# Fewer transfers for the remaining rows of a batch: six in place of ten

## The chip, the cores and the metric

One NeuronCore of a Trainium2 chip. The metric is device time in microseconds (us) of one execution of the whole program on that core. In the profile the engines are PE (TensorE, matmuls), PEld (its weight loads), DVE (VectorE), ACT (ScalarE), POOL (GpSimd) and SP (SyncE, which here only issues transfers). Each engine works through its own instruction list in order; SPq and ACTq are rows in which SP or ACT issues a transfer.

## The reference, cut to what matters

Three stages in a row, all in float32: sparse attention per head, a gated feed-forward layer, and a Fourier mixing with a channel network. B = 4 batches, S = 576 positions, D = 512 features.

```python
# attention: scores under (row maximum - tau) are dropped, softmax, times v
x = attn_out.transpose(0, 2, 1, 3).reshape(B, S, D)
# feed-forward ("FFN")
xk = mu_k * x + (1 - mu_k) * x_prev ; xr likewise with mu_r
k  = maximum(xk @ w_k, 0)
x  = sigmoid(xr @ w_r) * ((k * k) @ w_v)
# Fourier mixing and channel network
mixed = real(fft(fft(x, axis=1), axis=2))
u  = x + mixed
un = (u - mean(u)) / sqrt(var(u) + 1e-6)
out = u + maximum(un @ w_ch1, 0) @ w_ch2
```

## The kernel before

**Stages.** Attention runs to about 510 us of the profile. The FFN goes on behind it for the batches 2 and 3 until about 617 us (matmuls into `kps` with w_k, `rps` with w_r, `vps` with w_v), and beside it run the Fourier stages of batches 0 and 1. From about 617 us on the channel network (`mixer`, matmuls into `c1ps` and `c2ps`) fills PE, and beside it run the Fourier stages of batches 2 and 3.

**The Fourier stage of one batch.** The FFN's output lies in DRAM as `xd[b]`, 577 rows of 512 floats: row s holds position s up to 287, row 288 + s holds the mirror position 576 - s, and row 576 (again in row 288) the middle position 288. `fft_fold(b)` loads a row and its mirror row to the same partition of two tiles. Two pairs of 128 rows come by `load_pairs` (tiles `xa`, `xb`). What is left, 32 rows and the middle row, comes by `load_rem` into two tiles `ra` and `rb` of 98 partitions each: the 32 rows stand there three times (partitions 0 to 31, 33 to 64 and 65 to 96) and the middle row twice (32 and 97), since one matmul of 98 rows then takes the high and low parts of data and table at once. `folded` makes sums and differences of them: ACT copies `fp<-ra` (L776) and `fq<-rb` (L777), and adds on DVE (L778 to L781). `stack_tile` rounds them into `ske` and `sko`: ACT L793, DVE L794. In `stage_1` (`fft_one`), the matmuls with the cosine table `tc1` and the sine table `ts1` (L802 to L804) collect into `f`, and the matmul L805 with `ske` or `sko` closes each sum. The tables are loaded by POOL (L746) at the start of batch 0.

**What sets the order.** The program is written as generators that are interleaved (`side` next to the FFN, `behind` next to the mixer). The order on each engine is then set by a scheduler that goes by priorities and its own estimate of when operands are there. So a change of a few transfers also moves rows on PE, DVE, ACT and SP that have nothing to do with them. All engines are in order: an ACT row that waits for a transfer holds up all ACT rows behind it. The c1ps, kps, rps and vps sums share two PSUM buffers (`psm`); each is emptied by an ACT row: `relu` (L473) for kps, `hh` (L1100) for c1ps.

**Queues and lanes.** `xa`, `xb`, `ra`, `rb` and the reloads of the mixer are issued by SP; the channel weights `wraw` (L56) and the FFN's stores `xd<-xnat` (L558) by ACT. Transfers of SP and ACT share eight completion counters, called lanes here (DMAHW0 to DMAHW7 in the order listings). Before a transfer is issued, the issuing engine waits for the transfer that used the same lane before.

**Buffers.** `ra` and `rb` take two of the four buffers with tag "o"; the normed inputs `un` and the FFN's `xnat` are in the same four. In batch 2, the tiles must wait until the transposes of `un` on PE (L1005) have read theirs.

Of the kernel before, what the change touches and what calls it, by code (L numbers as in the profile page):

```python
# [20 lines left out]
D, FF, FC = 512, 1024, 2048  # L21
# [8 lines left out]
def tile_kernel(ctx: ExitStack, tc: tile.TileContext, a):  # L30
    nc = tc.nc
    pe, dve, act, pool, sp = nc.tensor, nc.vector, nc.scalar, nc.gpsimd, nc.sync
# [5 lines left out]
    xd = [dram.tile([S + 1, D], F32, name=f"xd{b}") for b in range(B)]  # L38
# [722 lines left out]
    def load_rem(b):  # L761

        xa = chp.tile([128, D], F32, tag="o", bufs=4, name="ra")[:98]
        xb = chp.tile([128, D], F32, tag="o", bufs=4, name="rb")[:98]
        for r in (0, 33, 65):
            sp.dma_start(xa[r:r + 32], xd[b][256:288, :])
            sp.dma_start(xb[r:r + 32], xd[b][544:576, :])
        for r in (32, 97):
            sp.dma_start(xa[r:r + 1], xd[b][576:577, :])
            sp.dma_start(xb[r:r + 1], xd[b][576:577, :])  # L770
        return xa, xb

    def folded(xa, xb, n):
# [76 lines left out]
    def fft_fold(b):  # L850
        while written[b] < 2:
            yield
        settle()
        prs = prs_of[b] = load_pairs(b)
        ra, rb = load_rem(b)
        parts_e, parts_o = [], []
        for xa, xb in prs:
            e, o = folded(xa, xb, 128)
            yield
            parts_e.append(split_tile(e, 257, "fse"))  # L860
            parts_o.append(split_tile(o, 256, "fso"))
            yield
        e, o = folded(ra, rb, 98)
        yield
        ske = stack_tile(e, 257, "ske")
        sko = stack_tile(o, 256, "sko")
        fold_of[b] = (parts_e, parts_o, ske, sko)
        yield
# [495 lines left out]
```

## Time and profile before

| | us |
|---|---|
| median of 3 runs | 1053.23 |
| the three runs | 1051.57 to 1055.49 |
| profiled execution, time | 1055.04 |
| profiled execution, span | 1053.0 |
| granted TensorE clock, mean | 0.989 |
| PE busy in the span | 1003.0 (95%) |
| DVE, ACT, POOL busy | 717.3, 536.3, 395.4 |

The span is what the trace covers; 2.04 us lie around it. Times within the trace count from the span's start. "Granted clock" is 1.00 where TensorE runs at the upper of its two levels (2.4 GHz) and 0.50 at the lower (1.2 GHz). Rows of SPq and ACTq are issues of transfers, not the transfers; where a transfer ends is read from who waited for it.

### The profile page before, as it was taken

The numbers are of one execution on the slowest core, as the hardware profiler recorded it, in microseconds if no ns is written. First come the engines' busy times: TensorE is split into PE (matmuls) and PEld (weight loads), VectorE is DVE, ScalarE is ACT, GpSimd is POOL, SyncE is SP. The second block draws the span as 40 slices with busy tenths as digits, with TensorE's granted clock in tenths as the row PEclk, the third lists the DMA queues.
The fourth block names the chain that finished last, engine by engine and source line by source line (L and its number), as shares of the span: only waits on it lengthen the run. The fifth ranks groups of instructions, "written<-read, shape, count | busy, mean of one in ns | idle before, by whom it ended". The sixth has DMA issues, their size and how long they took to land.

```text
span 1053.0 us, 18827 instructions
## 1 busy us (share of the span) xinstructions
PE 1003.0 (95%) x6807; PEld 884.1 (84%) x6807; DVE 717.3 (68%) x1880; ACT 536.3 (51%) x1211; POOL 395.4 (38%) x495
## 2 busy tenths in 40 slices
PE   6887779999999999999999989999999999999998
PEld 4565659988889888999889879898998888889997
DVE  6799988667776685865356889457537449236776
ACT  4688777675866766857265745243313113113332
POOL 1445868465584564844233100000014125112231
PEclk9899989999999999999999989999999999999999
DMA  6442332121211212100613666536325335223221
GB/s 228 146 133 80 118 108 60 48 67 43 72 60 48 73 31 88 51 24 14 198 55 110 202 204 200 159 127 207 119 92 180 130 119 175 96 101 120 101 100 61
DMA packets 45636, 114.52 MB, mean 109 GB/s; under 512 B 6319, under 2 KB 6740, under 8 KB 45544
## 3 DMA queue, kind: packets, MB, share of 16 engines
q1 hardware_dynamic: 27920, 74.47, 22.2%
q10 hardware_dynamic: 12344, 22.13, 6.8%
q0 software_dynamic: 5280, 16.72, 4.4%
q8 instruction: 54, 0.88, 0.4%
q14 instruction: 38, 0.31, 0.1%
HBM read 84.98 MB, written 28.32 MB: 108 GB/s over the span
## 4 chain that ended last, share of the span: by engine, by line
PE 74%; DVE 10%; DMA 6%; ACT 3%; issue 3%; POOL 2%; SPq 0%; ACTq 0%; DVEq 0%; POOLq 0%
PE c1ps L1090 7%; PE c1ps L1089 6%; PE c1ps L1088 6%; PE s L227 5%; PE av L388 5%; PE c2ps L1112 5%; PE c2ps L1110 5%; PE c2ps L1111 5%; PE p L1045 4%; PE t L329 4%; PE kps L408 2%; PE kps L409 2%; PE kps L410 2%; DMA rawqk<-in_qk 2%; PE vps L530 2%
## 5 line engine op out<-in xcount | busy, mean ns | idle before, releaser
L267 DVE TENSOR_REDUCE small<-s 128x1 f32<-128x576 f32 x144 | 106.9, 752 | 48.1 <-PE s L227 37.3
L1159 POOL DMA_DIRECT2D ud<-u x54 | 29.5, 546 | 264.2 <-DVE u L1158 206.3
L290 POOL TENSOR_SCALAR e<-e,small 128x576 f32<-128x576 f32 x112 | 90.1, 811 | 87.9 <-DVE small L637 73.5
L282 DVE SCALAR_TENSOR_TENSOR e<-s,small,e 128x576 f32<-128x576 f32 x128 | 102.7, 812 | 25.6 <-ACT e L278 22.4
L278 ACT ACTIVATE e<-s,small 128x576 f32<-128x576 f32 x128 | 93.9, 745 | 31.1 <-DVE small L267 27.9
L1100 ACT ACTIVATE hh<-c1ps 128x256 fp32r<-128x256 f32 (+1 forms) x84 | 37.1, 443 | 137.2 <-PE c1ps L1090 111.6
L1101 DVE SCALAR_TENSOR_TENSOR hh<-c1ps,hh 128x256 fp32r<-128x256 f32 (+1 forms) x84 | 41.6, 496 | 89.2 <-ACT hh L1100 89.2
L329 PE MATMUL t<-ident,e 128*128 128x128 f32 x512 | 82.5, 278 | 12.9 <-ACT pt L332 6.5
L332 ACT ACTIVATE pt<-t 128x512 f32<-128x512 f32 x128 | 75.2, 599 | 22.3 <-PE t L329 20.6
L329 PEld LDWEIGHTS t<-ident,e 128*128 128x128 f32 x512 | 61.2, 142 | 24.3 <-issue 6.9
L488 POOL TENSOR_TENSOR k<-relu,k 128x288 fp32r<-128x288 f32 x64 | 54.3, 851 | 68.1 <-ACT k L486 63.9
L408 PE MATMUL kps<-xh,wk 128*128 128x288 f32 x256 | 78.1, 306 | 1.7 <-DVE tg L537 0.9
L530 PE MATMUL vps<-k,wv 128*128 128x288 f32 x256 | 77.5, 304 | 0.4 <-ACT tg L518 0.4
L531 PE MATMUL vps<-k,wv 128*128 128x288 f32 x256 | 77.3, 303 | 0.0
L532 PE MATMUL vps<-k,wv 128*128 128x288 f32 x256 | 76.7, 301 | 0.0
L410 PE MATMUL kps<-xh,wk 128*128 128x288 f32 x256 | 76.2, 298 | 0.0
L409 PE MATMUL kps<-xl,wk 128*128 128x288 f32 x256 | 76.2, 298 | 0.0
L1090 PE MATMUL c1ps<-ut,cB 128*128 128x256 f32 (+1 forms) x256 | 76.0, 297 | 0.0
L1089 PE MATMUL c1ps<-ut,cB 128*128 128x256 f32 (+1 forms) x256 | 75.8, 296 | 0.0
L1088 PE MATMUL c1ps<-ut,cB 128*128 128x256 f32 (+1 forms) x256 | 75.7, 296 | 0.0
L1088 PE MATMUL c1ps<-ut,cA 128*128 128x256 f32 (+1 forms) x224 | 71.0, 317 | 1.4 <-ACT ut L1008 1.4
L1089 PE MATMUL c1ps<-ut,cA 128*128 128x256 f32 (+1 forms) x224 | 70.7, 316 | 0.0
(270 smaller groups left out, 3116.4 us busy)
## 6 DMA issues: line engine op xcount, KB each, us to landing
u<-ud SPq DMA_DIRECT2D x36, 512.0 KB
wraw<-in_w_ch ACTq DMA_DIRECT2D x64, 256.0 KB
rawqk<-in_qk SPq DMA_DIRECT2D x24, 608.0 KB
ud<-u POOLq DMA_DIRECT2D x54, 256.0 KB, 2.5
v<-in_v SPq DMA_DIRECT2D x16, 320.0 KB
un<-ud SPq DMA_DIRECT2D x18, 256.0 KB
out<-u SPq DMA_DIRECT2D x18, 256.0 KB
wraw<-in_w_k SPq DMA_DIRECT2D x8, 512.0 KB
```

The costliest lines, as they stand in the source:

```text
L267: dve.tensor_reduce(st[:, 0:1], sps[n][:, :, 0:HS], axis=AX.XY, op=ALU.max, negate=True)
L278: act.activation(two(eview(n)), sps[n][:, :, 0:HS], AF.Exp, bias=st[:, 0:1])
L282: dve.scalar_tensor_tensor(e, sps[n][:, :, 0:HS], st[:, 1:2], e, op0=ALU.is_ge, op1=ALU.mult, accum_out=st[:, 2:3])
L290: pool.tensor_scalar(e, e, st[:, 2:3], 1.0, op0=ALU.mult, op1=ALU.mult)
L329: pe.transpose(t[:, k, :], e[:, o + 128 * k:o + 128 * (k + 1)], ident)
L408: pe.matmul(ps, wh, x[0][k], start=(k == 0), stop=False)
L409: pe.matmul(ps, wh, x[1][k], start=False, stop=False)
L410: pe.matmul(ps, wl, x[0][k], start=False, stop=(k == nk - 1))
L530: pe.matmul(ps, wv[0][:, c:c + 128], k2[0][:, k, :], start=(k == 0), stop=False)
L1088: pe.matmul(ps, wh, ut[0][:, k, :], start=(k == 0), stop=False)
L1089: pe.matmul(ps, wh, ut[1][:, k, :], start=False, stop=False)
L1090: pe.matmul(ps, wl, ut[0][:, k, :], start=False, stop=(k == 3))
```

## The change

In `load_rem` the ten transfers per batch become six. For each of `ra` and `rb` one transfer fills the partitions 33 to 96: it reads the 32 source rows twice, through an access pattern whose first dimension has two steps of stride zero. One fills the partitions 0 to 31 as before. One fills the partitions 32 and 97 with the middle row, again through a pattern that repeats its source twice. The bytes that arrive are the same: 98 rows of 2 KB in each tile. All three transfers of `ra` are now issued ahead of those of `rb`; before, they alternated.

```diff
         xa = chp.tile([128, D], F32, tag="o", bufs=4, name="ra")[:98]
         xb = chp.tile([128, D], F32, tag="o", bufs=4, name="rb")[:98]
-        for r in (0, 33, 65):
-            sp.dma_start(xa[r:r + 32], xd[b][256:288, :])
-            sp.dma_start(xb[r:r + 32], xd[b][544:576, :])
-        for r in (32, 97):
-            sp.dma_start(xa[r:r + 1], xd[b][576:577, :])
-            sp.dma_start(xb[r:r + 1], xd[b][576:577, :])
+        for x, r in ((xa, 256), (xb, 544)):
+            rows = xd[b][r:r + 32, :]
+            sp.dma_start(x[33:97], rows.rearrange("(a p) d -> a p d", a=1).to_broadcast([2, 32, D]))
+            sp.dma_start(x[0:32], rows)
+            sp.dma_start(x[32:98:65], xd[b][576:577, :].to_broadcast([2, D]))
         return xa, xb
```

The file is one line shorter, and in the listings of the order after the change every line from L768 of before on has a number that is lower by one: L776 is L775, L805 is L804, L1100 is L1099.

On ACT in batch 0, from the issue of a weight load on, with what each row waits for (DMAHW: a lane; PE, DVE, Pool, Activation: a counter of that engine). Before:

```order
L56 DMA wraw<-in_w_ch 128x512 [waits DMAHW4_49,DMAHW2_49,DVE_49]
L777 ACTIVATE fq<-xb 128x2 [waits DMAHW7_49]
...
L473 ACTIVATE relu<-kps 128x288 [waits PE_49]
L556 ACTIVATE xnat<-xn 128x512 [waits PE_49]
L479 ACTIVATE relu<-relu 128x288 [waits Activation_49]
L558 DMA xd_65<-xnat 128x512 [waits DMAHW4_49,Activation_49]
L486 ACTIVATE k_6363<-relu 128x288 [waits Activation_49]
L776 ACTIVATE fp<-ra 98x2 [waits DMAHW5_49,DMAHW7_49,DMAHW1_49,DMAHW0_49]
L473 ACTIVATE relu<-kps 128x288 [waits PE_49,Pool_49]
L479 ACTIVATE relu<-relu 128x288 [waits Activation_49]
L777 ACTIVATE fq<-rb 98x2 [waits DMAHW6_49,DMAHW3_49,DMAHW0_49]
```

With the change:

```order
L56 DMA wraw<-in_w_ch 128x512 [waits DMAHW7_49,DMAHW4_49,DVE_49]
L776 ACTIVATE fq<-xb 128x2
...
L473 ACTIVATE relu<-kps 128x288 [waits PE_49]
L775 ACTIVATE fp<-ra 98x2 [waits DMAHW3_49,DMAHW1_49,DMAHW0_49]
L556 ACTIVATE xnat<-xn 128x512 [waits PE_49]
L479 ACTIVATE relu<-relu 128x288 [waits Activation_49]
L558 DMA xd_65<-xnat 128x512 [waits Activation_49]
L486 ACTIVATE k_6359<-relu 128x288 [waits Activation_49]
L776 ACTIVATE fq<-rb 98x2 [waits DMAHW6_49,DMAHW5_49,DMAHW4_49]
L473 ACTIVATE relu<-kps 128x288 [waits PE_49,Pool_49]
L479 ACTIVATE relu<-relu 128x288 [waits Activation_49]
L792 ACTIVATE ske<-fy 98x257 [waits DVE_49]
```

The weight load no longer waits for lane 2, which in the order before carries the third transfer of `ra` and `rb`, but for lane 7, which carries a transfer of `xb`. `fp<-ra` has moved ahead of an eviction (xnat), and `fq<-rb` ahead of the next relu eviction of kps.

On PE in batch 0, behind the second group of transposes `xn<-ident,tg`. Before (24 kps matmuls stand between, of which the last three are shown):

```order
L408 MATMUL kps<-xh,wk_86 128x288
L409 MATMUL kps<-xl,wk_86 128x288
L410 MATMUL kps<-xh,wk_87 128x288
L805 MATMUL f_6503<-tc1r,ske 128x290
L805 MATMUL f_6513<-ts1r,sko 128x288
```

With the change:

```order
L548 MATMUL xn<-ident,tg 128x128 x4
L804 MATMUL f_6499<-tc1r,ske 128x290
L408 MATMUL kps<-xh,wk_86 128x288
L409 MATMUL kps<-xl,wk_86 128x288
L410 MATMUL kps<-xh,wk_87 128x288
...
L804 MATMUL f_6509<-ts1r,sko 128x288
L408 MATMUL kps<-xh,wk_86 128x288
```

The matmul with `ske` has moved ahead by 24 kps matmuls, to directly behind the transposes; that with `sko` by 12.

On ACT in batch 2, from the copies of the transposed `un` on (`ut`; `cB<-wbits` rounds a weight piece). Before:

```order
L1008 ACTIVATE ut_7808<-ut 128x4x128 [waits PE_49] x2
L75 ACTIVATE cB_7703<-wbits 128x256 [waits DVE_49]
L56 DMA wraw<-in_w_ch 128x512 [waits DMAHW2_49,DMAHW0_49]
L1100 ACTIVATE hh<-c1ps 128x256 [waits PE_49,Activation_49]
L987 ACTIVATE lnst<-lnst 128x2 [waits DVE_49,Activation_49]
L75 ACTIVATE cB_7703<-wbits 128x256 [waits DVE_49]
L56 DMA wraw<-in_w_ch 128x512 [waits DMAHW6_49,DMAHW1_49]
L1100 ACTIVATE hh<-c1ps 128x256 [waits PE_49]
L776 ACTIVATE fp<-ra 98x2 [waits DMAHW4_49,DMAHW5_49,DMAHW3_49,DMAHW1_49]
L75 ACTIVATE cB_7703<-wbits 128x256 [waits DVE_49]
L56 DMA wraw<-in_w_ch 128x512 [waits DMAHW0_49]
L777 ACTIVATE fq<-rb 98x2 [waits DMAHW7_49,DMAHW5_49,DMAHW3_49]
```

With the change:

```order
L1007 ACTIVATE ut_7800<-ut 128x4x128 [waits PE_49] x2
L775 ACTIVATE fp<-ra 98x2 [waits DMAHW5_49,DMAHW4_49,DMAHW3_49]
L1099 ACTIVATE hh<-c1ps 128x256 [waits PE_49,Activation_49]
L986 ACTIVATE lnst<-lnst 128x2 [waits DVE_49,Activation_49]
L776 ACTIVATE fq<-rb 98x2 [waits DMAHW7_49,DMAHW6_49,DMAHW0_49]
L75 ACTIVATE cB_7695<-wbits 128x256 [waits DVE_49]
L56 DMA wraw<-in_w_ch 128x512 [waits DMAHW2_49]
L75 ACTIVATE cB_7695<-wbits 128x256 [waits DVE_49]
L56 DMA wraw<-in_w_ch 128x512 [waits DMAHW1_49]
L1099 ACTIVATE hh<-c1ps 128x256 [waits PE_49]
```

`fp<-ra` now stands directly behind the copies of `ut`; before, two evictions `hh` came first. `fq<-rb` has one `hh` ahead of it in place of two.

## Rows read from the trace of the kernel before

**Rows 1.** The page, part 1: busy us (share) x instructions

```profile
PE 1003.0 (95%) x6807; PEld 884.1 (84%) x6807; DVE 717.3 (68%) x1880; ACT 536.3 (51%) x1211; POOL 395.4 (38%) x495
```

**Rows 2.** PE in time order, batch 0, idle time before in brackets

```profile
523.02 0.37 PE L802 MATMUL f<-ts,fsoh 128*128 128x288 f32 x1 [1.51 <-DMA ts<-in_ts]
...
526.00 0.41 PE L802 MATMUL f<-tc,fseh 128*128 128x290 f32 x1 [0.31 <-ACT fseh L787]
...
527.50 0.40 PE L804 MATMUL f<-ts,fsol 128*128 128x288 f32 x1 [0.34 <-DVE fsol L788]
...
531.66 0.40 PE L408 MATMUL kps<-xh,wk 128*128 128x288 f32 x1
...
534.95 0.29 PE L805 MATMUL f<-tc1r,ske 98*128 98x290 f32 x1
```

**Rows 3.** The chain of work, 505 us on: start us, us, what

```profile
513.74 4.91 DMA ra<-xd
518.65 5.34 issue
```

**Rows 4.** Stretches: us, engines' busy us, PEclk, DMA share, GB/s

```profile
510.00:527.00 17.00, 15.18 (x111) 14.50 (x109) 8.25 (x23) 3.95 (x14) 4.71 (x8) 1.00 1.10 313
...
617.00:624.00 7.00, 5.38 (x24) 5.09 (x25) 5.42 (x13) 4.01 (x9) 0.00 (x0) 0.51 0.98 327
640.00:660.00 20.00, 20.00 (x132) 18.19 (x131) 17.95 (x59) 9.03 (x23) 1.08 (x2) 1.00 0.75 220
...
527.00:528.00 1.00, 0.66 (x5) 0.50 (x4) 0.45 (x1) 0.92 (x3) 0.17 (x1) 1.00 0.11 36
512.00:514.00 2.00, 2.00 (x17) 2.00 (x16) 0.26 (x1) 0.21 (x1) 2.00 (x4) 1.00 1.07 386
```

**Rows 5.** The tile ra: its issues on SP, ns min/median/max

```profile
L766 SPq DMA_DIRECT2D ra<-xd x12: 302/414/487, 511.7 to 650.3; - x12
```

**Rows 6.** ACT in time order, batch 0: start us, us, line, out<-in

```profile
528.13 0.19 ACT L776 ACTIVATE fp<-ra 98x2 f32<-98x2 f32 x1
...
530.39 0.19 ACT L777 ACTIVATE fq<-rb 98x2 f32<-98x2 f32 x1
```

**Rows 7.** DVE in time order, batch 0

```profile
532.84 0.42 DVE L794 TENSOR_TENSOR ske<-fy,ske 33x257 fp32r<-33x257 f32 x1 [0.27 <-ACT ske L793]
```

**Rows 8.** SP's queue in time order, batch 2

```profile
639.07 1.25 SPq L766 DMA_DIRECT2D ra<-xd  x3
```

**Rows 9.** The page, part 6: KB each, us from issue to landing

```profile
ud<-u POOLq DMA_DIRECT2D x54, 256.0 KB, 2.5
```

**Rows 10.** ACT in time order, batch 2

```profile
640.17 0.60 ACT L1008 ACTIVATE ut<-ut 128x512 fp32r<-128x512 f32 x1 [0.53 <-PE ut L1005]
...
646.06 0.20 ACT L776 ACTIVATE fp<-ra 98x2 f32<-98x2 f32 x1
...
646.46 0.20 ACT L777 ACTIVATE fq<-rb 98x2 f32<-98x2 f32 x1
```

**Rows 11.** PE in time order, batch 2

```profile
646.51 0.28 PE L1088 MATMUL c1ps<-ut,cA 128*128 128x256 f32 x1
...
648.86 0.28 PE L1088 MATMUL c1ps<-ut,cA 128*128 128x256 f32 x1
...
657.22 0.30 PE L805 MATMUL f<-tc1r,ske 98*128 98x290 f32 x1
```

**Rows 12.** SP in time order, batch 1

```profile
539.22 0.21 SPq L770 DMA_DIRECT2D rb<-xd  x1
```

**Rows 13.** ACT in time order, batch 1

```profile
564.20 0.21 ACT L776 ACTIVATE fp<-ra 98x2 f32<-98x2 f32 x1 [0.23 <-DVE fsel L788]
```

**Rows 14.** ACT in time order, batch 3

```profile
690.11 0.19 ACT L776 ACTIVATE fp<-ra 98x2 f32<-98x2 f32 x1
```

**Rows 15.** PE in time order, end of the FFN

```profile
615.13 0.76 PE L548 MATMUL xn<-ident,tg 128*128 128x128 f32 x5 [1.43 <-DVE tg L537]
...
618.20 0.58 PE L1088 MATMUL c1ps<-ut,cA 128*128 128x256 f32 x1 [1.45 <-ACT ut L1008]
```

## The prediction

> **What bounds the kernel now.** The first view was the page's first part: PE is busy 95% of the span, the next engine 68% [rows 1]. So a gain has to come from PE's idle time or its clock, and a loss is whatever makes PE wait. The change touches four places, one per batch, and I read PE in time order around each. At batch 0, three waits stand: 1.51 us for the sine table `ts`, 0.31 for `fseh`, 0.34 for `fsol` [rows 2]; the matmuls with `ske` at 534.95 follow their neighbours without a wait. The chain of work shows where the short ones come from: it runs through the third transfer of the remaining rows, from 513.74 for 4.91 us, and then 5.34 us of "issue" on ACT [rows 3]. By the listing of the order, that is the weight load L56 standing on lane 2 until this transfer has landed, at 518.65 + 5.34 = 523.99. All ACT work of the fold queues behind it, `fseh` and `fsoh` too. At batch 2 PE has no wait: all 20 us of 640 to 660 are busy [rows 4].
>
> **What is removed.** On SP an issue of 32 rows takes 0.41 us [rows 5]; four fewer per batch are 1.7 us at most. They lie on SP, which computes nothing, and PE waits for no issue in these stretches; I cost them at nothing. If issues did stand on the path, up to 1.7 us per batch would be the gain. The larger removal is the ACT wait: L56 now stands on a lane that a transfer of `xb` used, issued ahead of all these. That can give back 0.31 + 0.34 = 0.65 us in batch 0; the 1.51 for the table stay, since POOL's loads don't change.
>
> **What the new transfers cost.** No row of before shows a transfer that reads its source twice. The lower bound is that they run as the 32-row ones do, spread over all sixteen DMA engines: then the same bytes take the same time and the cost is nothing. The upper bound is that the dimension of two, which stands outermost in the 64-row and the 2-row patterns, is what is dealt out to the engines, so that only two of sixteen carry them. The weight is then not in the sum of bytes but in two queues: 64 rows x 2048 B = 131 kB per tile, 65.5 kB on each of the two engines, for both tiles 131 kB, plus 4 kB from the 2-row transfers and 8 from the 32-row ones, 143 kB. Before, these engines had a sixteenth of 196 x 2048 B, 25 kB. So 118 kB more on two engines. I take this bound, because the access pattern as written has nothing but the two to deal out in front, and the change put it there in place of a dimension of 32.
>
> The Trainium skill says the same as a rule: in "DMA: Bandwidth & Descriptors", section "Rules for kernel authors", a leading zero-stride broadcast of c copies confines the whole DMA to at most c engines. No row of before shows it, as said. Its row on many small transfers in the same section speaks for the change (below 64 KB mostly overhead); by that one the sum would be a gain of up to 1.7 us per batch if SP's issues were on the path, which no row here bears out.
>
> **Batch 0.** In 510 to 527 the DMA engines are saturated (share 1.10): 313 GB/s x 17 us = 5.32 MB, 333 kB per engine. At 527 they fall to 0.11 [rows 4]. Their rate when full: 386 GB/s / 16 = 24.1 kB per us and engine. The extra 118 kB keep two engines busy 118 / 24.1 = 4.9 us longer, and `rb`, last in SP's queue, lands at about 531.9; before, `fp<-ra` ran at 528.13 and `fq<-rb` at 530.39 [rows 6], when neither was waited for. From `fq<-rb` to the end of the low part of `ske` on DVE are 532.84 + 0.42 - 530.39 = 2.9 us [rows 6, 7]. So `ske` is ready at 534.8. In the new order PE wants it directly behind the transposes, where kps goes on at 531.66 in before [rows 2], and no longer at 534.95: the 24 kps matmuls (3.2 us) that would have covered the delay now stand behind it. PE loses 534.8 - 531.66 = **3.1 us**. The 0.65 us of the ACT wait are no separate gain then: PE would only reach the wait earlier. Behind the late `fp<-ra` stand the eviction `xnat`, and behind `fq<-rb` the next `relu`, so part of the loss will show as PE waiting for ACT. Bounds: -0.65 (sixteen engines) and about +6 (the clock falls as well, below).
>
> **Batch 2.** SP issues from 639.07 [rows 8]. A store of 256 KB over sixteen engines lands in 2.5 us [rows 9]; 16 kB at 24.1 are 0.7, which leaves 1.8 us from issue to landing beside the bytes. The DMA engines are at 0.75 there [rows 4]. If the two engines serve these bytes all of the idle quarter and half of the rest, they get 0.625 x 24.1 = 15 kB/us: 4.4 us for a tile, 8.7 for both. `ra` lands at 639.3 + 4.4 + 1.8 = 645.5, `rb` at 649.8. ACT in the new order reaches `fp<-ra` right behind the copies of `ut`, that is from 640.8 on, where before it came at 646.06 and `fq<-rb` at 646.46 [rows 10]. The first `hh` behind it comes out at about 646.1; PE needs its buffer for the third c1ps group at 646.51 [rows 11], so no loss. The second `hh` stands behind `fq<-rb` and two roundings `cB` of 0.42: 649.8 + 0.2 + 0.84 + 0.38 = 651.2, and the fourth group, which starts at 648.86 in before, must wait for it: **2.4 us**. `ske` itself is wanted at 657.22 [rows 11] and is no issue. Bounds: at the full rate `rb` lands at 646.5 and the loss is nothing; at half rate it is 4.5; if the two engines have only their idle quarter, 6 kB/us, it is about 15. The middle is nearest to the row on the share, so I take it.
>
> **Batches 1 and 3, and the order.** Batch 1's last transfer is issued at 539.22 [rows 12] and `ra` used at 564.20 [rows 13]; batch 3's last 32-row transfer of `ra` is issued at 650.3 [rows 5] and `ra` used at 690.11 [rows 14]. Even 15 us more are covered there; without this cover the price would be that of batch 2 each. The scheduler also reorders DVE and ACT at the end of the FFN. There PE waits 1.43 us for `tg` and 1.45 for `ut` [rows 15], and behind these waits the granted clock is 0.51 for 7 us with 5.38 us of PE work [rows 4]; at full clock the same work takes 5.38 x 0.51 = 2.7, so 2.6 us are lost. DVE's last `tg` has about seven operations fewer ahead of it, but batch 1's `make_u` runs later; I set this at 0, with -5.5 (1.43 + 1.45 + 2.6) and +3 as bounds.
>
> **Sum.** 3.1 + 2.4 + 0 = +5.5 us. Against the profiled execution, whose 1055.04 us are its 1053.0 of span and 2.04 around it, that is 1060.5. The median of the three runs lies 1.81 below the profiled one, so I state the time against it: 1053.23 + 5.5 = **1058.7 us**.
>
> **The rivals.**
> - *No cost, no gain.* The new transfers are spread over all sixteen engines like the old, or the two engines' queue is hidden. For it: no row of before shows the confinement, and batches 1 and 3 have cover. Against: the new order takes the cover away in batches 0 and 2. Gain 0.65: 1052.6.
> - *Faster, through the wait for `tg`.* Transfers cost nothing and the reordering brings `tg` 1.43 us or more earlier at 613. The point that decides is whether the idle time before 617 shrinks enough that the clock stays at 1.00 as it does behind the 1.51 us wait at 523 [rows 2, 4]. Then 0.65 + 1.43 + 1.45 + 2.6 = 6.1 us are gained: 1047.1. Against: later `make_u` rows on the same engine.
> - *Slower by more.* The two engines, and in batch 0 the waits for the table and for `ra` and `rb` add up to where the clock falls as at 617 (+2.6), or batch 2 runs at half rate or less (4.5 and more in place of 2.4). 1058.7 + 2.6 + 2.1 = 1063.4, and up to 1071 at a quarter of the rate.
>
> **Chances.** A difference of 0.5%, 5.3 us, is about what a measurement of this kernel can tell from none: 1047.9 and 1058.5 are the limits. The forecast's case (two engines, 1054 to 1062) has 0.50, of which 0.21 lie under the limit; no cost 0.19; the gain at `tg` 0.12, of which 0.10 under 1047.9; slower by more 0.19. Faster 0.10, same 0.21 + 0.19 + 0.02 = 0.42, slower 0.29 + 0.19 = 0.48. The range that leaves out most of the `tg` case and the end of the last case is 1050 to 1066.
>
> **What would show it.** Right: in batch 0 PE waits 2 to 4 us in the stretch 527 to 535 for `ske`, `xn` or kps, released by ACT or by `ra`/`rb`; ACT shows idle time before `fp<-ra` or `fq<-rb`, released by their transfers, in batch 0 and in batch 2; DMA share behind 527 stays small but above zero (two of sixteen is 0.12) until about 532; the 5.34 us of "issue" are gone. Wrong: if ACT runs `fp<-ra` of batch 2 right behind `ut` without a wait, the transfers aren't confined and the first rival holds. If the transfers are late and PE still doesn't wait, the cover is larger than I read it. If the stretch 612 to 624 differs by more than 3 us, the order decides and not the transfers.

## The result and the profile after

| | before | after |
|---|---|---|
| median of six runs each, us | 1053.82 | 1065.40 |
| lowest to highest, us | 1051.57 to 1055.49 | 1062.53 to 1067.73 |
| ratio, 95% interval | | 1.0109 [1.0089, 1.013] |
| profiled execution: time, span, us | 1055.04, 1053.0 | 1067.73, 1065.8 |
| granted clock, mean | 0.989 | 0.985 |

The change costs 11.5 us (0.0109 x 1053.8), more than twice the 5.5 that were forecast. In the runs below, one execution of e7 (3436.52 us) and one of e8 (2503.97 us) are slow ones and are left out of medians and ratios. The profiled execution is the slowest of the six, and 12.8 us longer in its span than that of before, of which 6.5 are more busy time of PE [rows 1]; the number of matmuls is the same.

```profile
PE 1009.5 (95%) x6807; PEld 887.1 (83%) x6807; DVE 715.4 (67%) x1880; ACT 535.9 (50%) x1211; POOL 395.7 (37%) x495
```

The chain of work from 505 us on shows the new wait. Where [rows 3] had 4.91 us of a transfer and 5.34 of "issue", `rb` now holds the chain for 13.43 us, down to the fold:

```profile
510.99 7.75 DMA wraw<-in_w_ch
518.75 13.43 DMA rb<-xd
...
532.31 0.42 DVE fp L777
```

The stretches after, and then those of before (us, busy us of PE, PEld, DVE, ACT, POOL, PEclk, DMA share, GB/s):

```profile
520.00:525.00 5.00, 4.09 (x32) 3.88 (x31) 3.20 (x7) 2.07 (x7) 0.81 (x1) 1.00 1.24 316
525.00:530.00 5.00, 2.73 (x23) 2.50 (x20) 0.00 (x0) 1.10 (x4) 0.00 (x0) 1.00 0.37 108
530.00:535.00 5.00, 2.95 (x18) 2.26 (x18) 2.38 (x7) 3.09 (x10) 1.41 (x2) 1.00 0.23 76
535.00:540.00 5.00, 5.00 (x26) 5.00 (x27) 1.38 (x3) 2.97 (x8) 1.40 (x3) 0.66 0.31 104
527.00:528.00 1.00, 0.72 (x6) 0.49 (x4) 0.00 (x0) 0.00 (x0) 0.00 (x0) 1.00 0.14 49
...
536.00:538.00 2.00, 2.00 (x10) 2.00 (x10) 0.20 (x1) 0.49 (x3) 0.80 (x1) 0.50 0.56 179
...
650.00:651.00 1.00, 0.04 (x1) 0.04 (x1) 0.06 (x1) 0.57 (x3) 0.00 (x0) 1.00 0.13 49
664.00:666.00 2.00, 2.00 (x14) 1.53 (x12) 1.71 (x6) 0.47 (x2) 0.00 (x0) 1.00 0.11 38
668.00:672.00 4.00, 3.05 (x14) 3.01 (x14) 3.85 (x9) 0.41 (x1) 1.08 (x2) 0.57 1.00 282
```

```profile
520.00:525.00 5.00, 3.49 (x27) 3.29 (x26) 0.72 (x2) 0.60 (x3) 0.00 (x0) 1.00 1.34 291
525.00:530.00 5.00, 4.35 (x29) 3.72 (x29) 3.18 (x6) 3.48 (x10) 1.61 (x2) 1.00 0.60 179
530.00:535.00 5.00, 4.88 (x38) 4.64 (x37) 2.66 (x6) 4.48 (x13) 1.60 (x2) 1.00 0.39 118
535.00:540.00 5.00, 5.00 (x40) 4.80 (x40) 1.28 (x3) 3.77 (x12) 1.61 (x2) 1.00 0.15 33
```

Three things are to be seen. From 527 to 528, and from 650 to 651 in batch 2, the transfer engines are 0.14 and 0.13 busy and move 49 GB/s: two of sixteen (0.125), at some 24 GB/s each. PE is busy 14.77 us of 520 to 540, where it was 17.72: 2.95 less. And from 535 to 540 it is busy throughout, but at 0.66 of its clock; the stretch 536 to 538 lies at 0.50, the lower level. That gives away 5 x 0.34 = 1.7 us more. The sum, 4.6, is what a fixed point behind it shows: the first matmul into `rps` starts at 547.79 and not at 543.16 (0.26 of it was there before batch 0: a `vps` row at 516.93 stood at 516.67).

PE in time order, with the idle time before a row and its releaser:

```profile
529.99 0.41 PE L408 MATMUL kps<-xh,wk 128*128 128x288 f32 x1 [2.27 <-ACT xnat L556]
...
532.85 0.66 PE L548 MATMUL xn<-ident,tg 128*128 128x128 f32 x4 [0.99 <-ACT relu L473]
534.49 0.40 PE L804 MATMUL f<-tc1r,ske 98*128 98x290 f32 x1 [0.99 <-DVE ske L793]
...
620.29 0.77 PE L548 MATMUL xn<-ident,tg 128*128 128x128 f32 x5 [0.65 <-DVE tg L537]
...
623.36 0.38 PE L1087 MATMUL c1ps<-ut,cA 128*128 128x256 f32 x1 [1.45 <-ACT ut L1007]
...
650.96 0.50 PE L1109 MATMUL c2ps<-cA,hh 128*128 128x512 f32 x1 [1.29 <-ACT hh L1099]
...
654.50 0.50 PE L1109 MATMUL c2ps<-cA,hh 128*128 128x512 f32 x1 [0.45 <-ACT hh L1099]
...
655.70 0.39 PE L1087 MATMUL c1ps<-ut,cA 128*128 128x256 f32 x1 [0.46 <-DVE hh L1100]
...
659.25 0.50 PE L1109 MATMUL c2ps<-cA,hh 128*128 128x512 f32 x1 [0.89 <-DVE u L1157]
...
667.54 0.50 PE L1087 MATMUL c1ps<-ut,cA 128*128 128x256 f32 x2 [1.17 <-ACT ut L1007]
...
668.99 0.61 PE L801 MATMUL f<-tc,fseh 128*128 128x290 f32 x1 [0.95 <-DVE ut L1008]
...
670.60 0.45 PE L804 MATMUL f<-tc1r,ske 98*128 98x290 f32 x1
```

In batch 2, where PE had no wait [rows 4], there are now six of 0.45 us and more, 5.2 us in all, and none is for `ra`, `rb` or `ske` itself. ACT says where the first of them come from:

```profile
529.25 0.21 ACT L775 ACTIVATE fp<-ra 98x2 f32<-98x2 f32 x1 [3.90 <-DMA ra<-xd]
...
532.29 0.21 ACT L776 ACTIVATE fq<-rb 98x2 f32<-98x2 f32 x1 [1.50 <-DMA rb<-xd]
...
650.43 0.21 ACT L775 ACTIVATE fp<-ra 98x2 f32<-98x2 f32 x1 [6.38 <-DMA ra<-xd]
650.54 0.36 ACT L1099 ACTIVATE hh<-c1ps 128x256 fp32r<-128x256 f32 x1
...
653.19 0.21 ACT L776 ACTIVATE fq<-rb 98x2 f32<-98x2 f32 x1 [2.19 <-DMA rb<-xd]
```

ACT stands for 6.38 us at `fp<-ra`, and an `hh` that PE needs stands right behind it. Between the first `c1ps` of the mixer and the first `ske` matmul of batch 2 lie 670.60 - 623.36 = 47.2 us; before, 657.22 - 618.20 = 39.0 [rows 11, 15]. So this execution lost 8.2 us between these two rows, and 4.6 around batch 0; together that is the 12.8 of the span. Not all of the 8.2 are batch 2's own, as e5 and e6 show below.

### The profile page after: what moved, and what is told of

The parts are those of the page before. It is cut to its first block, busy times and chain, and to the rows that moved or that the text cites. A ratio compares the mean times of both kernels' runs of the same rounds, so it can differ in the third digit from the quotient of the medians.

```text
span 1065.8 us, 18794 instructions
## 1 busy us (share of the span) xinstructions
PE 1009.5 (95%) x6807; PEld 887.1 (83%) x6807; DVE 715.4 (67%) x1880; ACT 535.9 (50%) x1211; POOL 395.7 (37%) x495
## 4 chain that ended last, share of the span: by engine, by line
PE 69%; DVE 12%; DMA 9%; ACT 4%; issue 3%; POOL 2%; SPq 0%; ACTq 0%; DVEq 0%; POOLq 0%
PE c1ps L1089 6%; PE c1ps L1087 6%; PE c1ps L1088 6%; PE av L388 5%; PE s L227 5%; PE c2ps L1109 4%; PE c2ps L1111 4%; PE c2ps L1110 4%; PE p L1044 4%; PE t L329 4%; DMA wraw<-in_w_ch 3%; PE kps L408 2%; PE kps L410 2%; PE kps L409 2%; DMA rb<-xd 2%
## 5 line engine op out<-in xcount | busy, mean ns | idle before, releaser
L1100 DVE SCALAR_TENSOR_TENSOR hh<-c1ps,hh 128x256 fp32r<-128x256 f32 (+1 forms) x84 | 41.6, 495 | 96.9 <-ACT hh L1099 96.8
L1099 ACT ACTIVATE hh<-c1ps 128x256 fp32r<-128x256 f32 (+1 forms) x84 | 37.1, 442 | 137.6 <-PE c1ps L1089 114.4
L329 PE MATMUL t<-ident,e 128*128 128x128 f32 x512 | 82.7, 279 | 10.5 <-ACT pt L332 4.6
L408 PE MATMUL kps<-xh,wk 128*128 128x288 f32 x256 | 79.0, 309 | 3.9 <-ACT xnat L556 2.4
L531 PE MATMUL vps<-k,wv 128*128 128x288 f32 x256 | 77.3, 303 | 0.0
L1087 PE MATMUL c1ps<-ut,cB 128*128 128x256 f32 (+1 forms) x256 | 75.7, 296 | 0.0
L1088 PE MATMUL c1ps<-ut,cB 128*128 128x256 f32 (+1 forms) x256 | 75.5, 295 | 0.0
L1087 PE MATMUL c1ps<-ut,cA 128*128 128x256 f32 (+1 forms) x224 | 70.9, 317 | 3.1 <-ACT ut L1007 2.6
L1088 PE MATMUL c1ps<-ut,cA 128*128 128x256 f32 (+1 forms) x224 | 70.6, 315 | 0.0
```

The source lines that it names most:

```text
L329: pe.transpose(t[:, k, :], e[:, o + 128 * k:o + 128 * (k + 1)], ident)
L408: pe.matmul(ps, wh, x[0][k], start=(k == 0), stop=False)
L1087: pe.matmul(ps, wh, ut[0][:, k, :], start=(k == 0), stop=False)
L1088: pe.matmul(ps, wh, ut[1][:, k, :], start=False, stop=False)
```

## The experiments

The first theory was: the transfers with the dimension of two in front run on two engines, which makes `ra` and `rb` late, and all else follows. Its rivals: the new order of the rows costs by itself, since it puts PE's and ACT's waiting rows earlier; or batch 2 alone carries the loss. The kernels e1 to e6 change only what the six transfers read (and in e1 the order of the tables' rows); PE runs exactly the order of the changed kernel, row by row.

**e1: the same six transfers, rows in front, copies inside.** The tables are laid out to match.

```diff
-            sp.dma_start(x[33:97], rows.rearrange("(a p) d -> a p d", a=1).to_broadcast([2, 32, D]))
+            sp.dma_start(x[33:97], rows.rearrange("p (a d) -> p a d", a=1).to_broadcast([32, 2, D]))
...
-        return np.concatenate([hi, last, hi, lo, last], 0)
+        pair = np.stack([hi.reshape(32, 1, -1), lo.reshape(32, 1, -1)], 1).reshape(64, -1)
+        return np.concatenate([hi, last, pair, last], 0)
```

> The six transfers, with the 64-row one written so that the 32 rows stand outermost and the two copies inside; copy and original of a row now lie on neighbouring partitions, and the constant tables tc1r and ts1r are laid out to match, so the same sums are made. Every engine's row order is that of the changed kernel. Theory (the transfers sit on two DMA engines): ra and rb of batch 2 land 2 to 3 us after issue in place of 7 to 8, ACT waits for neither, and the time is back near before, 1050 to 1055. Rival (the new order of rows costs): same order, so 1063 to 1067. Rival (a source that is read twice is slow however it is dealt out): 1062 or more.

Measured: 1055.15, ratio 1.0009 [0.9998, 1.002]. With the same order and the same number of transfers the loss is gone but for 0.9 us, which isn't clear of nothing. On ACT the waits are gone in batch 0 and short in batch 2:

```profile
525.68 0.20 ACT L775 ACTIVATE fp<-ra 98x2 f32<-98x2 f32 x1
...
527.17 0.19 ACT L776 ACTIVATE fq<-rb 98x2 f32<-98x2 f32 x1
...
640.49 0.21 ACT L775 ACTIVATE fp<-ra 98x2 f32<-98x2 f32 x1 [2.56 <-DMA ra<-xd]
```

**e2 and e3: four and eight in front.** The 64 rows are 16 rows read four times, and 8 rows read eight times.

```diff
-            sp.dma_start(x[33:97], rows.rearrange("(a p) d -> a p d", a=1).to_broadcast([2, 32, D]))
+            sp.dma_start(x[33:97], xd[b][r:r + 16, :].rearrange("(a p) d -> a p d", a=1).to_broadcast([4, 16, D]))
```

> As the changed kernel in order and bytes, but the 64-row transfer reads 16 rows four times in place of 32 rows twice, so that the outermost dimension is four; rows 16 to 31 of the copies are left out and the output differs. Theory: the load per engine is halved (33 kB per tile), batch 0 keeps about 2 of its 4.9 us of extra queue, which the way to ske covers, and in batch 2 rb lands about 5 us after issue: 1054 to 1058. Rival (order) and rival (source read more than once): no less than the changed kernel, 1063 to 1067.

> As the changed kernel in order and bytes, but the 64-row transfer reads 8 rows eight times, so that the outermost dimension is eight; rows 8 to 31 of the copies are left out and the output differs. Theory: 16 kB per engine and tile; over the interleaved kernel two engines cost 10, four cost 3.3, eight 0 to 1.5: 1055 to 1057. If something other than the engines' load grows with the number of repeats of a source row, it is slower than with four.

Measured: four 1.0043 [1.0028, 1.0059], eight 1.0008 [0.9993, 1.0022]. The loss over e1 goes 10.5, 3.6, 0 us for two, four and eight in front. It follows the size of the leading dimension, and eight are already as good as the rows themselves. A source that is read more often isn't slower by that: e3 reads each of its rows eight times.

**e4, e5, e6: two in front in some batches only**, e1's transfers in the others (e5 and e6 with `b == 2` and `b % 2` in the same place):

```diff
-            sp.dma_start(x[33:97], rows.rearrange("(a p) d -> a p d", a=1).to_broadcast([2, 32, D]))
+            sp.dma_start(x[33:97], rows.rearrange("(a p) d -> a p d", a=1).to_broadcast([2, 32, D]) if b == 0 else rows.rearrange("p (a d) -> p a d", a=1).to_broadcast([32, 2, D]))
```

> The changed kernel's transfers in batch 0 alone; in batches 1 to 3 the 64-row one has the rows outermost as in the first experiment, so those batches' copies stand in another order than the table and their output differs. Same row order everywhere. Theory: batch 0 costs 4 to 5 us by the lag of PE behind before (3 by the wait for ske, 1.5 to 2 by the clock behind it): 4 to 5 over the first experiment. Rival (batch 0 is only the place where it shows, the order costs): equal to the first experiment.

> The changed kernel's transfers in batch 2 alone; the copies of batches 0, 1 and 3 stand in another order than the table and their output differs. Same row order everywhere. Theory: batch 2 costs 7 to 9 us, half of it directly by ACT and DVE rows that stand behind fp<-ra, fq<-rb and hh, half later by the transposes that come late and the clock: 7 to 9 over the first experiment. My prediction had it at 2.4. If the loss of batch 2 needs the delay of batch 0 ahead of it, it is 2 to 3.

> The changed kernel's transfers in batches 1 and 3 alone, the interleaved ones in 0 and 2, same row order everywhere; in batches 0 and 2 the copies stand in another order than the table and their output differs. Theory: 25 to 40 us of cover hide them, so the time is that of the interleaved kernel within 1 us, 1054 to 1056. Rival (two engines that carry 143 kB hold up every other transfer that is spread over all sixteen, used or not): 2 to 5 us over the interleaved kernel.

| | ratio | interval | us over e1 |
|---|---|---|---|
| e4, batch 0 | 1.0049 | 1.0032 to 1.0067 | 4.2 |
| e5, batch 2 | 1.0048 | 1.0033 to 1.0064 | 4.1 |
| e6, batches 1 and 3 | 1.0024 | 1.0007 to 1.004 | 1.6 |
| all four (the change) | 1.0109 | 1.0089 to 1.013 | 10.5 |

The last column is the difference of ratios times 1053.8. The parts add to 9.9 of the 10.5. Batch 0 and batch 2 carry it in equal parts, so the rival that batch 2 alone does it has fallen; the intervals of e6 and e1 overlap, so the 1.6 of the covered batches isn't clear of nothing. For batch 2 the expectation was too high.

The profiles tell more than the times, since PE runs the same rows in the same order in all these kernels. The start of one row can be subtracted from kernel to kernel (us; the lag behind e1 in brackets):

| PE row | e1 | the change | e4 | e5 | e6 |
|---|---|---|---|---|---|
| a `vps` (L531) ahead of batch 0 | 516.61 | 516.93 (0.32) | 514.12 (-2.49) | 518.23 (1.62) | 516.47 (-0.14) |
| the first `rps` (L408) behind batch 0 | 541.77 | 547.79 (6.02) | 543.48 (1.71) | 543.11 (1.34) | 541.25 (-0.52) |
| a `c1ps` (L1087) ahead of the waits for `hh` | 643.03 | 649.15 (6.12) | 645.12 (2.09) | 646.13 (3.10) | 643.25 (0.22) |
| a `c2ps` (L1110) behind them | 655.15 | 664.90 (9.75) | 656.74 (1.59) | 661.65 (6.50) | 654.95 (-0.20) |
| a `c1ps` (L1088) behind the waits for `ut` | 659.54 | 672.62 (13.08) | 661.05 (1.51) | 665.90 (6.36) | 662.27 (2.73) |

The changed kernel loses 5.7 us in batch 0 (e4: 4.2), 3.6 in the waits for `hh` and `u` (e5: 3.4), and 3.3 in the waits for `ut` behind them. That last loss isn't in e5; it is in e6, with 2.9, where batch 2's transfers are e1's. So it comes from batch 3's transfers. SP issues them from 653.97 to 657.5 in the changed kernel and from 643.25 to 646.8 in e6, and while they stand in the queue of two engines, a weight load `wraw` comes late. The same DVE row in the changed kernel, in e6 and in e5:

```profile
664.29 0.29 DVE L69 TENSOR_SCALAR wbits<-wraw 128x256 int32<-128x256 int32 x1 [2.21 <-DMA wraw<-in_w_ch]
...
653.64 0.29 DVE L69 TENSOR_SCALAR wbits<-wraw 128x256 int32<-128x256 int32 x1 [1.51 <-DMA wraw<-in_w_ch]
...
658.76 0.28 DVE L69 TENSOR_SCALAR wbits<-wraw 128x256 int32<-128x256 int32 x1
```

It has no wait in e1 to e4 either, though other rows wait for `wraw` there (in e1 0.81 us at 655.01). From 664 to 666 the transfer engines are 0.11 busy in the changed kernel, as by two that still work. Behind this row stand the weight pieces `cB` and `ut`, and PE waits for `ut` as in the changed kernel. In e6, and then the one wait that e5 has there:

```profile
656.89 0.50 PE L1087 MATMUL c1ps<-ut,cA 128*128 128x256 f32 x2 [0.61 <-ACT ut L1007]
...
658.41 0.57 PE L801 MATMUL f<-tc,fseh 128*128 128x290 f32 x1 [1.02 <-DVE ut L1008]
```

```profile
663.55 0.41 PE L801 MATMUL f<-tc,fseh 128*128 128x290 f32 x1 [0.35 <-DVE ut L1008]
```

The clock fell behind these waits, to a mean of 0.57 from 668 to 672 in the changed kernel and from 658 to 662 in e6; in e5 it is 1.00 from 663 to 667:

```profile
658.00:662.00 4.00, 3.58 (x15) 3.59 (x16) 3.28 (x7) 0.41 (x1) 1.08 (x2) 0.57 0.97 282
...
663.00:667.00 4.00, 3.65 (x29) 3.45 (x29) 3.70 (x8) 0.83 (x2) 1.08 (x2) 1.00 1.04 302
```

This is the rival of e6's expectation (other transfers are held up), seen in two profiled executions. How much it costs on average isn't settled by the 1.6.

**e7: before's ten transfers, nearly in its order, but four of them on two engines.** Of the three 32-row transfers of each tile, two read 16 rows twice with the two in front. The diff is against the kernel before.

```diff
         for r in (0, 33, 65):
-            sp.dma_start(xa[r:r + 32], xd[b][256:288, :])
-            sp.dma_start(xb[r:r + 32], xd[b][544:576, :])
+            sp.dma_start(xa[r:r + 32], xd[b][256:272, :].rearrange("(a p) d -> a p d", a=1).to_broadcast([2, 16, D]) if r else xd[b][256:288, :])
+            sp.dma_start(xb[r:r + 32], xd[b][544:560, :].rearrange("(a p) d -> a p d", a=1).to_broadcast([2, 16, D]) if r else xd[b][544:576, :])
```

> The kernel before, with its ten transfers and nearly its row order (ske still behind 24 kps matmuls, fp<-ra of batch 2 behind three evictions hh), but two of the three 32-row transfers of a tile read 16 rows twice with the copies outermost, so that they sit on two engines; rows 16 to 31 of these copies are left out and the output differs. Theory (late transfers hurt because the new order took their cover away): PE waits 0 to 2 us in batch 0 and 0 to 2 in batch 2, in all 1055 to 1058. Rival (the two engines cost the same wherever the rows stand, by holding up ACT and DVE or other transfers): 1062 to 1066.

Measured: 1062.59, ratio 1.008 [1.0055, 1.0105]. This part of my theory fell: the old order costs 8.4 us with transfers on two engines, and its interval overlaps that of the changed kernel, with 11.5. In the profiled execution, the fastest at 1059.27, ACT waits at the same row, and PE behind it:

```profile
529.64 0.21 ACT L776 ACTIVATE fp<-ra 98x2 f32<-98x2 f32 x1 [1.64 <-DMA ra<-xd]
...
649.16 0.21 ACT L776 ACTIVATE fp<-ra 98x2 f32<-98x2 f32 x1 [4.66 <-DMA ra<-xd]
```

```profile
530.71 0.41 PE L408 MATMUL kps<-xh,wk 128*128 128x288 f32 x1 [2.47 <-ACT relu L473]
...
664.09 0.40 PE L802 MATMUL f<-tc,fseh 128*128 128x290 f32 x1 [2.09 <-DVE G L810]
```

With e1 this makes a table of two by two, in us over before: order before and sixteen engines 0; new order and sixteen 0.9; order before and two 8.4; new order and two 11.5. The transfers carry most of it; what the order adds, 0.9 alone and 3.1 with them, isn't clear of nothing by the intervals.

**e8: six interleaved transfers in the batches 0 and 1**, ten in 2 and 3 (into every second partition, to match the table):

```diff
+        if b < 2:
+            for x, r in ((xa, 256), (xb, 544)):
+                rows = xd[b][r:r + 32, :]
+                sp.dma_start(x[33:97], rows.rearrange("p (a d) -> p a d", a=1).to_broadcast([32, 2, D]))
...
+            for r in (slice(0, 32), slice(33, 97, 2), slice(34, 97, 2)):
```

> A candidate: six interleaved transfers in batches 0 and 1, ten of the old kind in 2 and 3 (into every second partition, tables laid out to match, same sums). By the lag of PE the interleaved kernel gained 1.2 us in batch 0 and lost 1.7 in batch 2, where the new order puts fp<-ra right behind the copies of ut; here batch 2 has two evictions hh ahead of it again. Theory: 1 to 2 us under the interleaved kernel, 1052 to 1054, about 0.1 to 0.2 percent under before. Rival (the lags are chance of the scheduler's other rows): 1054 to 1056.

Measured: 1053.29, ratio 0.9994 [0.9977, 1.0012]; no difference from before, nor a clear one from e1.

**e9: the changed kernel, with the fold of `ra` and `rb` of batch 2 on POOL.** If what costs in batch 2 is that ACT stands at `fp<-ra`, the loss there should go.

```diff
+        if apart:
+            for t, s in ((p, xa), (q, xb)):
+                pool.tensor_scalar(t[:n, 0:257:256], s[:, 0:257:256], 1.0, 1.0, op0=ALU.mult, op1=ALU.mult)
+        else:
...
+        eng = pool if apart else dve
...
-        e, o = folded(ra, rb, 98)
+        e, o = folded(ra, rb, 98, b == 2)
```

> The changed kernel with the fold of ra and rb of batch 2 (two copies, four sums) on POOL in place of ACT and DVE; transfers, their engines and their issue are as changed, and the ACT order is that of the changed kernel without its two rows fp<-ra and fq<-rb of batch 2. Theory (the loss of batch 2 comes from rows that stand behind the late fold on ACT and DVE, hh above all): two evictions hh come out in time, ACT first waits at ske, and batch 2 costs 2 to 4 us in place of about 8: 1059 to 1062. Rival (the sums with ske are what PE waits for, or the late transfers hold up other transfers): no change, 1064 to 1067, since ske comes no earlier.

Measured: 1064.28, ratio 1.0091 [1.0076, 1.0106]; above what was expected, and no clear difference from the changed kernel. POOL waits for the transfers now, and ACT waits for POOL at the next row that needs the fold, `ske`. The rows of POOL, ACT and PE in time order:

```profile
648.89 0.19 POOL L777 TENSOR_SCALAR fp<-ra 98x2 f32<-98x2 f32 x1 [7.13 <-DMA ra<-xd]
652.65 0.20 POOL L777 TENSOR_SCALAR fq<-rb 98x2 f32<-98x2 f32 x1 [3.57 <-DMA rb<-xd]
```

```profile
655.05 0.42 ACT L797 ACTIVATE ske<-fy 98x257 fp32r<-98x257 f32 x1 [5.90 <-POOL fy L784]
...
656.48 1.51 ACT L999 ACTIVATE un<-un,lnst 128x512 f32<-128x512 f32 x2
```

```profile
657.34 0.90 PE L1009 MATMUL ut<-ident,un 128*128 128x128 f32 x3 [4.28 <-ACT un L999]
```

The rows behind `ske` on ACT, here the normed inputs `un`, are held up in place of `hh`. PE doesn't wait for `ske`, it waits for what stands behind it. Batch 3's transfers stay on two engines here, and DVE's waits for `wraw` are there too (2.41 us at 652.35, 1.60 at 665.08).

**e10: e1 with the fold of the batches 2 and 3 on POOL** (e9's edit with `b > 1`).

> A candidate: the six interleaved transfers on sixteen engines in all batches, with the fold of ra and rb of batches 2 and 3 on POOL. Theory: the interleaved kernel's ACT still waited 2.6 us for ra and 1.2 for rb in batch 2, and PE lost 1.7 us there; without these rows on ACT and DVE 1 to 2 us are gained on it: 1052 to 1054. Rival (those 1.7 us are chance of the order): 1054 to 1056.

Measured: 1052.84, ratio 0.999 [0.9979, 1.0000]. PE's only wait from 640 to 658 is 0.20 us. Its ratio is the lowest of all, 0.1% under before; the interval reaches from 0.2% under to no change.

## Why the prediction was wrong

The sum was 3.1 for batch 0, 2.4 for batch 2 and nothing for the rest; over e1, the kernels with two in front in some batches cost 4.2, 4.1 and 1.6. Two steps failed: batch 2's term was too small, and the batches 1 and 3 were put at nothing because `ra` and `rb` are used late there, though their queue also delays other transfers.

**Two engines: right.** The dose in e1 to e3, and the shares of 0.14 and 0.13 at 527 and 650, show the confinement. The Trainium skill, in "DMA: Bandwidth & Descriptors", section "Rules for kernel authors", gives the leading copies of a broadcast as the upper limit of the engines that a transfer uses; the trace agrees, with 49 GB/s on two engines where the full set moved 386 [rows 4].

**The landings: right.** In batch 0 `rb` was to land at 531.9 and `ske` to be ready at 534.8; `fq<-rb` ran at 532.29 and the `ske` matmul at 534.49. In batch 2 SP issued 3.9 us later (643.00 against 639.07 [rows 8]), which shifts the forecast for `ra` and `rb` to 649.4 and 653.7; the ACT rows ran at 650.43 and 653.19. The share of the two engines that this rests on (all of the idle quarter, half of the rest) was a guess, so part of the fit is luck. The "issue" of 5.34 us is gone, as said. It bought nothing here; in e1 the first `rps` comes 1.4 us ahead of before (541.77 against 543.16).

**Batch 0: the stall right, the clock left out.** 3.1 us of waiting were forecast, 2.95 measured. The fall of the clock behind the waits stood only in the upper bound and among the rivals (2.6 us); in the profiled execution it came and cost 1.7. It doesn't come in each execution: e4's has PE waits of 2.01, 0.69 and 0.99 us in the same place and 1.00 behind them. Over e1, batch 0 costs 4.2 by the ratio and in e4's profile, which is some 2.8 over before, since e1 is ahead of before there.

**Batch 2: too small.** The prediction put the loss at 2.4 us, by asking when each `hh` empties its `c1ps` buffer. It measured 3.6 in the profiled execution over e1, and in e5 3.4 in the profile and 4.1 by the ratios. Three things were not in the sum. First, PE needs `hh` as an operand of `c2ps`, not only its buffer back: 1.29 and 0.45 us. Second, the first `hh` was taken to come just in time (646.1 against 646.51), a margin of 0.4 us under a landing that is known to about 1. Third, DVE stands at its half of `hh`, idle for 3.76 us in time order,

```profile
650.94 0.42 DVE L1100 SCALAR_TENSOR_TENSOR hh<-c1ps,hh 128x256 fp32r<-128x256 f32 x1 [3.76 <-ACT hh L1099]
```

and the weight pieces, the norm (`lnst`) and the adds into `u` queue behind it. They come out late one after the other, up to the wait for `u` of 0.89 at 659.25, 6 us after `rb` had landed. The waits for `ut` at 667.54 and 668.99 aren't part of this: e5 has all of the above and 0.35 us there. e9 shows the same from the other side: when the wait for the transfers left the two rows of the fold, it came back at `ske`, and 4.28 us of it reached PE.

**The order: nothing, as set.** e1 puts it at 0.9 us, not clear of zero. The wait for `tg` fell from 1.43 to 0.65 us [rows 15], the one for `ut` stayed at 1.45, and the lag grew only from 4.63 to 5.16 us between 547 and 623. The rival "faster through `tg`" found its shorter wait; of its gain by the clock there is a little (0.51 from 617 to 624 before [rows 4], a mean of 0.72 from 624 to 630 with the change), and none in the time. But the claim that the new order "takes the cover away" is wrong: in e7 the order before has as little.

**The covered batches: the step that failed; SP: right.** The prediction asked when `ra` of batch 3 is used, 40 us later [rows 5, 14], and put the loss at nothing. That wait is covered indeed. But 143 kB at 24.1 kB per us are a queue of 5.9 us on the two engines, and a weight load with no such cover came late in it. That cost 3.3 us in the profiled execution and 2.9 in e6's, of which the clock took 1.3 and 1.5 (3.05 and 3.58 busy us at 0.57). By the ratios the batches 1 and 3 cost 1.6, not clear of nothing. Four issues fewer saved little even on SP: by the medians of the tile's rows, six take 2 x (0.624 + 0.432 + 0.571) = 3.3 us per batch, and ten took 6 x 0.414 [rows 5] + 4 x 0.256 (last section) = 3.5.

```profile
L767 SPq DMA_DIRECT2D ra<-xd x4: 607/624/749, 511.9 to 654.0; - x4
L768 SPq DMA_DIRECT2D ra<-xd x4: 345/432/455, 513.6 to 654.6; - x4
L769 SPq DMA_DIRECT2D ra<-xd x4: 562/571/602, 515.1 to 655.1; - x4
```

**Still open.** The average cost of batch 3's queue, as said. Of the 8.2 us in the profiled execution, e1 with the same order has 1.6 over before between the same two rows (617.46 to 658.11, 40.65 us against 39.02). This and the gain in batch 0 nearly cancel in e1's time; which rows of the new order make them wasn't traced.

## What to carry to other kernels

When a transfer repeats its source, put the rows in front and the copies inside, and lay out what is multiplied with it to match; fewer transfers are worth nothing if they run on two engines. When a transfer comes late, price every row behind the one that waits for it, on that engine and on those that it feeds, and every other transfer that shares its transfer engines, even where the late data itself is wanted much later. Taking the wait to another engine doesn't help as long as an in-order engine meets the late data a few rows on. To tell a slow transfer from a new order, change only what the transfer reads, so that the order stays.

## What the runs showed of the hardware that was not expected

Eight in front were as good as 32 here (1.0008 and 1.0009), four were not (1.0043). A two-row transfer with a repeated source takes 0.571 us to issue on SP; before, the single-row ones took 0.256 at the median, so that one replaced two without a gain:

```profile
L769 SPq DMA_DIRECT2D ra<-xd x8: 215/256/302, 519.7 to 653.0; - x8
```

The granted clock fell to 0.50 at 536 to 538, after 2.27, 0.99 and 0.99 us of waiting; after the 2.01, 0.69 and 0.99 of e4 it didn't. Behind the waits for `ut` it fell after 1.17 and 0.95 us, and in e6 after 0.61 and 1.02.
